# Low words of w_out of the first token chunk's first six blocks read from the tile that made them

## The chip, the cores and the metric

The kernel runs on one core of one Trainium2 chip. The metric is device time in microseconds (us), the median of several executions. An instruction stream goes to each engine: TensorE (PE, its weight loads shown as PEld), VectorE (DVE), ScalarE (ACT), GpSimd (POOL) and SyncE (SP). SP issues every data transfer of this kernel, one after the other.

## The reference

Three layers in a row on 2304 tokens (4 batches of 576) and 512 features:

```
scores = q k^T / sqrt(64);  bias = -(cum[:, None] - cum[None, :]), cum = cumsum(max(s, 0))
x   = softmax(causal(scores + min(bias, 0))) v          # 8 heads of 64
x   = ((x @ w_a) * (x @ w_b)) @ w_out                   # 512 -> 1536 -> 512
out = relu(x @ w_in)^2 @ w_out2                         # 512 -> 2048 -> 512
```

The weights arrive as 64-bit numbers. The kernel turns each block of them into a 32-bit number and splits that into a high and a low word; a product is then the sum of three matmuls: high weight by high x, high weight by low x, low weight by high x.

## The kernel before, in words

**Tiling.** The 1536 hidden features of the middle layer are 12 blocks f of 128 (`NF1`), in four groups of three (`GRP = 3`, `NG = 4`). Tokens are cut into chunks; chunk 0 is the first 512 tokens, all of batch 0. `moe1(c)` lists the steps of a chunk: `fstep(f)` multiplies x by blocks f of w_a and w_b (PSUM tiles `ab`), multiplies both results and splits the product into g high and low. After each third block, `ystep(grp, z)`, z = 0 and 1, multiplies the three g of a group by the matching rows of w_out, for output features d = 2z and 2z + 1 (PSUM tile `py`, nine matmuls for each d, three of them with low words). All fsteps and ysteps of chunk 0 run while attention of batch 1 runs, and their matmuls lie between its score (`st`), transpose (`pt`) and value (`av`) matmuls.

**Making the weights.** Just ahead of `fstep(f)` of chunk 0, `split_w(f)` loads the raw words of the blocks f of w_a, w_b and w_out (512 KB each, into five lent raw buffers, shown as roomxh, roomxl, words), decodes them on ACT, DVE and POOL, and writes the high words to a tile `wh` that stays for later chunks. The low words go to a tile too, and from there to memory: w_a's and w_b's to `wlab`, w_out's in two transfers of 128 KB to `wlo[g][z]` (lines 988 to 991). Later chunks load them from there.

**Where low words live.** The tag `wh` is a ring of 36 tiles (`3 * NF1`, line 962). The 36 high tiles keep theirs. On loan from it until all are made are: the low tiles of w_a and w_b of f < 5 (`LF`), the low tiles of w_out of f < 6 (`LF1 = 6`, line 971), and one decode tile for each of the first nine blocks of w_out (line 975). That is 36 + 10 + 6 + 9 = 61 takings, and they are served strictly in the order of first use: the 37th needs one tile back, the 61st needs 25 back. In chunk 0, `fstep` reads the low words of w_a and w_b from the tile that `split_w` made (`first_lo`); `ystep` does not, it loads w_out's low words back from `wlo` into a `loo` tile of 384 KB (two buffers), lines 1061 and 1062.

**What sets the order.** Nothing is ordered by hand. Every step only adds operations with reads and writes; `Plan.order` (line 148) then simulates the engines with fixed costs and writes out one order for each. A load costs 3 ns for each KB on its one transfer clock, 560 ns of SP's time, and its data count as there 2000 ns after its end (`LATE`); SP is let at most 3000 ns ahead of that transfer clock (`QUEUE`). PE prefers attention of batch 1 (stream `next`) to chunk 0's steps (`moe`). Where it sees PE idle, it fills in dummy matmuls: up to 40 named `glow`, and before a bank that waits over 400 ns some on that bank (`op.idle`, shown as L256). Each engine then runs its list strictly in order and waits where something is late.

Of the kernel before, what the change touches and what calls it, by code (L numbers as in the profile page):

```python
# [7 lines left out]
F32 = mybir.dt.float32  # L8
F32R = mybir.dt.float32r
# [7 lines left out]
P = 128  # L17
# [246 lines left out]
def attention_moe_moe(tc, q, k, v, s, w_a, w_b, w_out, w_in2, w_out2, out):  # L264
# [12 lines left out]
    GRP = 3  # L277
# [10 lines left out]
    LF1 = 6  # L288
# [28 lines left out]
    def pool(name):  # L317
        return lambda: pools[name]
# [4 lines left out]
    def sb(shape, dtype, tag, bufs, name):  # L323
        return pl.tile(pool("sb"), shape, dtype, tag, bufs, name)

    def at(shape, dtype, tag, bufs, name):
        return gated("at", shape, dtype, tag, bufs, name)

    def scratch(shape, dtype, name):
        return pl.fixed(lambda: pools["dram"].tile(shape, dtype, name=name))  # L330

    def mm_bank(name):
        return pl.tile(pool("mm"), [P, 512], F32, "mm", 3, name)
# [23 lines left out]
    def dve(*args, reads=(), **kw):  # L357
        pl.call(on_dve(*args, **kw), reads=reads)

    def act(*args, **kw):  # L360
        pl.call(on_act(*args, **kw))
# [4 lines left out]
    def dma(out, in_, kb, takes=(), lag=0.0):  # L366
        pl.call(("SP", kb * 3.0, False, "dma_start", (out, in_), {}), takes=takes, lag=lag)
# [26 lines left out]
    wlo = [scratch([HD, P, 2, GRP, P], F32, f"wlo{g}") for g in range(NG)]  # L394
# [420 lines left out]
    def new_x(nm):  # L815
        ts = [sb([P, ND, W], F32R, t, 1, f"{t}{nm}") for t in ("xh", "xl")]
        return lambda d, o, n: [t[:, d, o : o + n].part((d, o)) for t in ts]

    def split_x(x, d, o, n, pieces):

        xh, xl = x(d, o, n)
        for at_, m, src in pieces:
            dma(xl[:, at_ : at_ + m].bitcast(F32), src, m * 0.5)
        copy(n, xh, xl.bitcast(F32))
        subtract(n, xl, xl.bitcast(F32), xh.bitcast(F32))
# [31 lines left out]
    def decode(w, by_col, f, hi, lo, raw, t, takes, by):  # L857

        words(w, by_col, f, raw, t, takes)
        n = ND * P  # L860
        hi, lo = (x.rearrange("p d c -> p (d c)") for x in (hi, lo))
        copy(n, hi, t.bitcast(F32), by="A")
        subtract(n, lo, t.bitcast(F32), hi.bitcast(F32), by=by)
# [85 lines left out]

        quarters(w_out2, False, j, temp, "w2o", send, apart)  # L950

    wh, first_lo = {}, {}
    more = [at([P, 2, S], I32, "T1", NT1, f"words{i}").rearrange("p i s -> p (i s)")[:, : 2 * DM] for i in range(NT1)]
    room = [sb([P, ND, W], I32, t, 1, f"room{t}").rearrange("p d s -> p (d s)") for t in ("xh", "xl")]
    W8 = 2 * DM
# [3 lines left out]
    def split_w(f):  # L959
        def g():  # L960
            def spare(i):
                return sb([P, ND, P], F32R, "wh", 3 * NF1, f"wl{f}_{i}")

            ab = None if f < LF else sb([P, 2, ND, P], F32R, "lo", 3, f"wl{f}")
            first_lo[f] = []
            for i, w in enumerate((w_a, w_b, w_out)):
                hi = sb([P, ND, P], F32R, "wh", 3 * NF1, f"wh{f}_{i}")
                if i < 2:
                    lo = ab[:, i].part(i) if ab else spare(i)
                else:  # L970
                    lo = spare(i) if f < LF1 else sb([P, ND, P], F32R, "lo1", 1, f"wlo{f}")
                k_ = 3 * f + i
                t = ts[k_ % 2]
                if f < 9:
                    t = sb([P, DM], I32, "wh", 3 * NF1, f"wt{f}_{i}") if i == 2 else ts[i]
                lent = [*raws, *more] if k_ < MORE else raws
                decode(w, i < 2, f, hi, lo, lent[k_ % len(lent)], t, (), "PD")
                wh[f, i] = hi
                if i < 2:
                    first_lo[f].append(lo)  # L980
                    if f < LF:
                        dma(wlab[f][:, i].part(i), lo.bitcast(F32), 256, lag=LAG)
            if f >= LF:
                dma(wlab[f], ab.bitcast(F32), 512, lag=LAG)
            g_, r = divmod(f, GRP)
            for z in range(HD):
                dma(
                    wlo[g_][z][:, :, r, :].part((z, r)), lo[:, 2 * z : 2 * z + 2, :].bitcast(F32), 128, lag=LAG,
                )

        return g


    def halves(nm, dtype):
        t = sb([P, 2 * W], dtype, "g", GB, nm)
        return [t[:, z * W : z * W + W].part(z) for z in range(2)]
# [3 lines left out]
    def attended(d, l, r):  # L1000

        for b in range(B):
            g0, g1 = (FIRST if b == 0 else b * S), b * S + S
            a, z = max(l, g0), min(r, g1)
            if a < z:
                yield a - l, z - a, xd[b][0][d][:, a - g0 : z - g0].part(d)

    def moe1(c):
        steps = []
        t0, t1 = spans[c]  # L1010
        n = t1 - t0
        st = {}
        first_chunk = c == 0

        def load():
            if first_chunk:
                st["x"] = first_x
                return
            st["x"] = new_x(f"{c}")
            for d in range(ND):  # L1020
                split_x(st["x"], d, 0, n, list(attended(d, t0, t1)))

        steps.append(load)

        def fstep(f):
            def g():
                nm = f"{c}_{f}"
                if first_chunk:
                    lo = first_lo[f]
                else:  # L1030
                    lo = sb([P, 2, ND, P], F32R, "lo", 3, f"lo{nm}")
                    dma(lo.bitcast(F32), wlab[f], 512)
                gh, gl = (x[:, :n] for x in halves(f"g{nm}", F32R))
                st["g", f] = (gh, gl)
                pp = []
                for i in range(2):
                    ps = mm_bank(f"ab{nm}_{i}")[:, :n]
                    pairs = []
                    for d in range(ND):
                        xh, xl = st["x"](d, 0, n)  # L1040
                        li = lo[i][:, d, :] if first_chunk else lo[:, i, d, :]
                        pairs += [(wh[f, i][:, d, :], xh), (wh[f, i][:, d, :], xl), (li, xh)]
                    if f < PIECES:
                        for d in range(ND):
                            matmul(ps, n, pairs[3 * d : 3 * d + 3], d == 0)
                    else:
                        matmul(ps, n, pairs)
                    pp.append(ps)
                a_sb = sb([P, 512], F32, "a", 2, f"a{nm}")[:, :n]
                act("copy", n, a_sb, pp[0], psum=True)  # L1050
                pb = pp[1]
                dve("tensor_tensor", n, out=pb, in0=pb, in1=a_sb, op=ALU.mult)
                act("copy", n, gh, pb, psum=True)
                dve("tensor_tensor", n, out=gl, in0=pb, in1=gh.bitcast(F32), op=ALU.subtract)

            return g

        def ystep(grp, z):
            def g():
                nm = f"{c}_{grp}_{z}"  # L1060
                lo = sb([P, 2, GRP, P], F32R, "loo", 2, f"loo{nm}")
                dma(lo.bitcast(F32), wlo[grp][z], 384)
                for d in (2 * z, 2 * z + 1):
                    if grp == 0:
                        st["y", d] = sb([P, W], F32, f"y{d}", 1, f"y{nm}_{d}")[:, :n]
                    y = st["y", d]
                    ps = mm_bank(f"py{nm}_{d}")[:, :n]
                    pairs = []
                    for i in range(GRP):
                        f = grp * GRP + i  # L1070
                        gh, gl = st["g", f]
                        pairs += [(wh[f, 2][:, d, :], gh), (wh[f, 2][:, d, :], gl), (lo[:, d % 2, i, :], gh)]
                    matmul(ps, n, pairs)
                    if grp == 0:
                        copy(n, y, ps, psum=True)
                    else:
                        dve("tensor_tensor", n, out=y, in0=ps, in1=y, op=ALU.add)
                    if grp == NG - 1:
                        dma(yd[c][d].part(d), y, n * 0.5)

            return g


        for f in range(NF1):
            steps.append(fstep(f))
            if f == 0:
                steps.extend(tail)
                tail.clear()
            elif f % GRP == 0:
                steps.extend(ystep(f // GRP - 1, z) for z in range(HD))  # L1090
        last = [ystep(NG - 1, z) for z in range(HD)]
        (tail if t1 > (B - 1) * S - CC else steps).extend(last)
        return steps
# [506 lines left out]
```

## Time and profile before

| | |
|---|---|
| time, median of 3 executions | 1021.84 us (1020.78 to 1024.65) |
| the profiled execution's own time | 1023.91 us |
| its span, first to last instruction | 1022.1 us |
| PE busy | 1002.8 us, 98% |
| DVE, ACT, POOL busy | 735.5, 603.9, 322.3 us |
| transfers, hardware queue | 239.52 MB, 71.1% of 16 DMA engines' span |
| loads into `loo` in chunks 0 and later (384 KB each) | 24 |

Busy time counts each engine's own instructions. A wait row names the engine that idled, the instruction that it idled before, and whose event came last. In a timeline the bracket at a row's end is the idle time before it and what ended it. SPq is the stretch in which SP issues a transfer.

### The profile page before, as it was taken

The page shows a single profiled execution, that of the slowest core. Times are in us where ns is not written, and L with a number is a line of the kernel's source. Part 1 is how long each engine was busy: PE and PEld are TensorE (multiplying, and loading weights), DVE is VectorE, ACT ScalarE, POOL GpSimd, SP SyncE. Part 2 cuts the span into 40 slices and gives each one's busy share as a digit, 9 for nine tenths or more (in the row PEclk, how much of TensorE's full clock was granted, in tenths as well). Part 3 has the DMA queues.
Part 4 walks back from the last instruction along what each step waited for, and adds up shares of the span by engine and source line. Part 5 has one row for each costly group of instructions (what it writes and reads, how often), then busy time and mean ns, then how long its engine had stood idle before and what let it go on. Part 6 is the DMA issues. An engine that isn't in the chain of part 4 may idle for free.

```text
span 1022.1 us, 16764 instructions
## 1 busy us (share of the span) xinstructions
PE 1002.8 (98%) x5612; PEld 867.8 (85%) x5619; DVE 735.5 (72%) x1546; ACT 603.9 (59%) x1373; POOL 322.3 (32%) x293
## 2 busy tenths in 40 slices
PE   9999999999999999999999999999999999999997
PEld 5766777777777778788889999999999999999997
DVE  5878876756677765565697898688767755876566
ACT  6777886565777643343344544487565766657552
POOL 2243134325454622101122323323335212431123
PEclk9999999999999999999999999999999999999999
DMA  7458896558778667857666668499968876678664
GB/s 226 131 157 256 273 288 186 152 150 258 228 199 246 185 212 262 275 183 233 206 207 207 208 206 273 164 336 363 344 219 322 313 260 231 246 273 319 220 233 165
DMA packets 138006, 240.58 MB, mean 235 GB/s; under 512 B 21320, under 2 KB 91072, under 8 KB 137920
## 3 DMA queue, kind: packets, MB, share of 16 engines
q1 hardware_dynamic: 137920, 239.52, 71.1%
q8 instruction: 44, 0.72, 0.3%
q14 instruction: 42, 0.34, 0.1%
HBM read 181.42 MB, written 52.11 MB: 228 GB/s over the span
## 4 chain that ended last, share of the span: by engine, by line
PE 75%; DMA 5%; DVE 2%; SPq 1%; ACT 1%; issue 0%; DVEq 0%; ACTq 0%
PE ab L261 14%; PE pa L261 9%; PE py L261 8%; PE po_0t L261 6%; PE pw L261 5%; PE pc L261 5%; PE wa L261 4%; PE st L261 3%; PE av L261 3%; PE pt L261 3%; PE wc L261 2%; PE pb L261 2%; PE po_2b L261 2%; PE po_1b L261 2%; PE po_0b L261 2%; PE po_3b L261 2%
## 5 line engine op out<-in xcount | busy, mean ns | idle before, releaser
L261 ACT ACTIVATE e<-st,neg 120x336 f32<-120x336 f32 (+2 forms) x192 | 93.5, 492 | 28.5 <-DVE neg L261 26.6
L261 PE MATMUL py<-g,wh 128*128 128x512 f32 x288 | 92.0, 401 | 1.4 <-DVE y L261 1.2
L261 PE MATMUL ab<-xh,wh 128*128 128x512 f32 x192 | 77.4, 403 | 0.0
L261 PE MATMUL ab<-xh,lo 128*128 128x512 f32 x192 | 75.0, 391 | 0.0
L261 PE MATMUL ab<-xl,wh 128*128 128x512 f32 x192 | 75.0, 390 | 0.0
L261 PE MATMUL pt<-ident,e 120*120 120x120 f32 (+2 forms) x480 | 68.0, 268 | 0.8 <-DVE ph L261 0.4
L261 PEld LDWEIGHTS pt<-ident,e 120*120 120x120 f32 (+2 forms) x480 | 51.2, 133 | 20.2 <-issue 9.2
L261 DVE CUSTOM_DVE_ANT_0 st<-st,mask 96x96 f32<-96x96 f32 (+4 forms) x120 | 53.7, 453 | 20.0 <-PE st L261 18.2
L261 PE MATMUL ab<-x,wh 128*128 128x512 f32 x192 | 65.8, 424 | 0.8 <-ACT a L261 0.7
L261 PEld LDWEIGHTS py<-g,wh 128*128 128x128 f32 x288 | 53.3, 190 | 12.6 <-DVE y L261 1.6
L261 PE MATMUL av<-ph,val 120*64 120x240 f32 (+3 forms) x512 | 58.7, 360 | 0.0
L261 PE MATMUL st<-fk,fq 65*120 65x336 f32 (+2 forms) x192 | 56.3, 408 | 1.7 <-ACT e L261 1.7
L261 ACT COPY ph<-pt 120x360 f32<-120x360 f32 (+3 forms) x81 | 36.5, 459 | 35.9 <-PE pt L261 34.8
L261 PE MATMUL py<-g,loo 128*128 128x512 f32 x144 | 56.9, 395 | 0.0
L261 PEld LDWEIGHTS av<-ph,val 120*64 120x64 f32 (+1 forms) x512 | 31.1, 136 | 24.9 <-issue 12.4
L261 DVE COPY ph<-pt 120x360 f32<-120x360 f32 (+3 forms) x79 | 39.8, 514 | 16.2 <-PE pt L261 14.9
L261 DVE TENSOR_TENSOR ab<-ab,a 128x512 f32<-128x512 f32 x36 | 25.2, 701 | 33.3 <-PE ab L261 28.7
L261 PEld LDWEIGHTS ab<-xh,lo 128*128 128x128 f32 x192 | 36.0, 188 | 7.7
L261 ACT COPY a<-ab 128x512 f32<-128x512 f32 x36 | 21.1, 586 | 35.7 <-PE ab L261 35.6
L261 PEld LDWEIGHTS ab<-xh,wh 128*128 128x128 f32 x192 | 36.1, 188 | 6.4 <-issue 0.4
L261 PEld LDWEIGHTS ab<-x,wh 128*128 128x128 f32 x192 | 33.7, 189 | 9.2 <-ACT a L261 1.6
L261 PEld LDWEIGHTS ab<-xl,wh 128*128 128x128 f32 x192 | 36.2, 188 | 5.9
(692 smaller groups left out, 3098.4 us busy)
## 6 DMA issues: line engine op xcount, KB each, us to landing
w<-w2q SPq DMA_DIRECT2D x48, 896.0 KB, 6.7
lo<-wlab SPq DMA_DIRECT2D x36, 512.0 KB, 4.7
w2q<-w2ip SPq DMA_DIRECT2D x48, 256.0 KB, 4.2
w2s<-w2op SPq DMA_DIRECT2D x48, 256.0 KB, 4.6
loo<-wlo SPq DMA_DIRECT2D x24, 384.0 KB, 5.5
w2ir<-in_moe_w_in SPq DMA_DIRECT2D x16, 512.0 KB, 5.7
w2or<-in_moe_w_out SPq DMA_DIRECT2D x16, 512.0 KB, 4.3
ws_0t<-w2s SPq DMA_DIRECT2D x12, 512.0 KB
```

The lines of the kernel that those rows point to most:

```text
L261: getattr(eng, method)(*map(real, args), **{k: real(a) for k, a in kw.items()})
```

## The change

`split_w(f)` keeps the low tile of w_out of f < 6 in a list. In chunk 0 the two ysteps of groups 0 and 1 read their low words from these tiles; they make no `loo` tile and issue no load. Groups 2 and 3 of chunk 0, and all groups of later chunks, load as before. The transfers that write `wlo` stay.

```diff
-    wh, first_lo = {}, {}
+    wh, first_lo, first_out = {}, {}, {}
...
                 wh[f, i] = hi
+                if i == 2 and f < LF1:
+                    first_out[f] = lo
...
         def ystep(grp, z):
             def g():
                 nm = f"{c}_{grp}_{z}"
-                lo = sb([P, 2, GRP, P], F32R, "loo", 2, f"loo{nm}")
-                dma(lo.bitcast(F32), wlo[grp][z], 384)
+                near = first_chunk and grp * GRP + GRP <= LF1
+                if not near:
+                    lo = sb([P, 2, GRP, P], F32R, "loo", 2, f"loo{nm}")
+                    dma(lo.bitcast(F32), wlo[grp][z], 384)
...
-                        pairs += [(wh[f, 2][:, d, :], gh), (wh[f, 2][:, d, :], gl), (lo[:, d % 2, i, :], gh)]
+                        low = first_out[f][:, d, :] if near else lo[:, d % 2, i, :]
+                        pairs += [(wh[f, 2][:, d, :], gh), (wh[f, 2][:, d, :], gl), (low, gh)]
```

## Rows read from the trace of the kernel before

**Rows 1.** The page's first part: span, and each engine's busy time (share) and instructions.
```profile
span 1022.1 us, 16764 instructions
PE 1002.8 (98%) x5612; PEld 867.8 (85%) x5619; DVE 735.5 (72%) x1546; ACT 603.9 (59%) x1373; POOL 322.3 (32%) x293
```

**Rows 2.** PE's longest waits, 80 to 260 us: total us, times, longest.
```profile
PE st L261 <- ACT e L261: 3.8, 3, 2.1
PE st L261 <- DMA t2k<-T: 1.1, 1, 1.1
PE ab L261 <- ACT a L261: 0.7, 1, 0.7
```

**Rows 3.** Stretches: length, engines' busy us (instructions), PE clock, DMA share, GB/s.
```profile
97.00:102.00 5.00, 5.00 (x30) 3.19 (x31) 4.94 (x12) 4.07 (x9) 2.57 (x2) 1.00 1.02 333
120.00:140.00 20.00, 19.02 (x91) 13.63 (x91) 15.52 (x35) 14.28 (x32) 3.23 (x3) 1.00 0.98 306
240.00:245.00 5.00, 4.23 (x17) 3.54 (x18) 3.15 (x13) 4.53 (x14) 3.73 (x3) 0.76 0.51 173
```

**Rows 4.** SP's timeline: start, us, instruction, transfer.
```profile
92.80 0.48 SPq L261 DMA_DIRECT2D loo<-wlo  x1
...
121.98 0.86 SPq L261 DMA_DIRECT2D loo<-wlo  x2
...
123.81 0.40 SPq L261 DMA_DIRECT2D roomxh<-in_moe_w_b  x1
...
126.96 0.35 SPq L261 DMA_DIRECT2D roomxh<-in_moe_w_out  x1
```

**Rows 5.** SP's own waits, 117 to 128 us.
```profile
SPq L261 <- DMA wlo<-wl: 1.3, 1, 1.3
SPq L261 <- DMA loo<-wlo: 1.3, 2, 0.8
```

**Rows 6.** Transfers issued between 80 and 130 us: KB each, median us to landing.
```profile
loo<-wlo SPq DMA_DIRECT2D x4, 384.0 KB, 5.5
```

**Rows 7.** PE's timeline around groups 0 and 1 of chunk 0.
```profile
103.04 0.63 PE L261 MATMUL py<-g,wh 128*128 128x512 f32 x2
103.51 0.39 PE L261 MATMUL py<-g,loo 128*128 128x512 f32 x1
...
132.04 0.75 PE L261 MATMUL st<-fk,fq 65*120 65x288 f32 x2 [0.86 <-ACT e L261]
...
140.20 0.39 PE L261 MATMUL py<-g,loo 128*128 128x512 f32 x1
...
151.27 0.40 PE L261 MATMUL py<-g,loo 128*128 128x512 f32 x1
```

**Rows 8.** PE's groups, 117 to 142 us: count, busy us, mean ns, idle.
```profile
L261 PE MATMUL ab<-x,wl 128*128 128x512 f32 x24 | 9.5, 395 | 0.0
L261 PE MATMUL py<-g,loo 128*128 128x512 f32 x3 | 1.2, 395 | 0.0
L261 PE MATMUL glow<-warm 128*128 128x512 bf16 x3 | 1.0, 383 | 0.1
L256 PE MATMUL py<-warm 128*128 128x512 bf16 x2 | 0.6, 386 | 0.0
```

**Rows 9.** ACT's timeline in chunk 0.
```profile
130.99 0.68 ACT L261 ACTIVATE roomxh<-roomxh 128x512 f32<-128x512 f32 x1 [1.37 <-DMA roomxh<-in_moe_w_b]
131.56 0.33 ACT L261 ACTIVATE e<-st,neg 96x96 f32<-96x96 f32 x1
...
134.71 0.68 ACT L261 ACTIVATE roomxh<-roomxh 128x512 f32<-128x512 f32 x1 [1.17 <-DMA roomxh<-in_moe_w_out]
...
178.27 0.62 ACT L261 CAST wh<-roomxl 128x512 fp32r<-128x512 f32 x1
```

**Rows 10.** PE's timeline in chunk 1.
```profile
240.77 0.47 PE L261 MATMUL st<-T 66*120 66x456 f32 x1 [2.08 <-ACT e L261]
...
242.92 1.06 PE L261 MATMUL py<-g,wh 128*128 128x512 f32 x2
```

## The prediction

> **What bounds the kernel now.** I read the page's busy times first. PE works 1002.8 of 1022.1 us, so only 19.3 us are not PE's work [rows 1]. The change takes no matmul away; it can give back only idle time of PE, or dummy matmuls. The view of PE's waits comes next, cut to 80 to 260 us, where chunk 0 and the start of chunk 1 run: the three lines shown make 3.8 + 1.1 + 0.7 = 5.6 us, and nearly all of it is score matmuls (`st`) that wait for ACT's exponentials or for a transfer [rows 2]. No line of that view names `loo`. Then the stretches: from 97 to 102 us the transfers fill the DMA engines (share 1.02) and PE is busy 5.00 of 5.00; from 120 to 140 us the share is 0.98 and PE lacks 0.98 us [rows 3]. So the transfers are dense where the loads go, but only the second place shows at PE.
>
> **Part by part.** *The matmuls.* Two groups by four features d by three blocks are 24 matmuls that take their weights from another tile. In this very stretch a matmul with weights from `loo` has a mean of 395 ns, one with weights from a low tile on the ring, as `fstep` reads them, 395 ns too [rows 8]. Cost 0.
>
> *The loads themselves.* Four loads go, each 384 KB, 1.57 MB in all. The later one of group 0 is issued at 92.80 us and lands after a median of 5.5 us, at about 98.3; the first matmul that reads such a tile starts at 103.51 [rows 4, 6, 7]. The pair of group 1 is issued from 121.98 to 122.84 and lands by about 128.3; its first reader starts at 140.20 [rows 4, 6, 7]. So they are 5 and 12 us early, and what hides them is the matmuls of `fstep` and attention. Taking them away gives PE nothing directly.
>
> *What stands behind the loads.* SP issues in order. Ahead of group 1's pair SP waited 1.3 us for the `wlo` writes to land, which only these loads need, the pair took 0.86 us to issue, and later issues waited 1.3 us for `loo` loads to land [rows 4, 5]. Behind the pair stand w_b's raw words (123.81) and w_out's (126.96) [rows 4]. They could go up to 1.3 + 0.86 = 2.2 us and 2.2 + 1.3 = 3.5 us earlier, if their raw buffers are free by then, and they no longer share the engines with 2 x 384 KB, which at the 306 GB/s of that stretch is 2.6 us [rows 3]. ACT stood 1.37 us for w_b's words at 130.99; the exponentials of attention sit behind that instruction in ACT's list, and PE's score matmul at 132.04 idled 0.86 us for them [rows 7, 9]. Words that land 2.2 us earlier take the whole 1.37 us away, and with it the 0.86. Next late would be ACT's wait of 1.17 us for w_out's words at 134.71; no PE wait stands behind that one now, and the same shift moves it [rows 9]. Upper bound: the 0.86 and the five dummy matmuls in this stretch, which mark where the order expected PE idle, 1.0 + 0.6 us busy, so 2.5 us [rows 7, 8]. Lower bound 0, if the buffers come free no earlier. I take the row itself, 0.86. Behind group 0's loads PE was fully busy, so I count nothing there.
>
> *The ring.* The six low tiles stay taken until the last matmul of their group instead of until their write to `wlo` has landed. Up to block 8 the ring is served by the nine decode tiles and the ten low tiles of w_a and w_b. Block 9 ends with the 55th taking and needs 19 back, just these 19. Block 10 ends with the 58th, needs 22, and so must have group 0's three. Block 11's first high tile is the 59th, needs 23, and so must wait for group 1's last matmul, which starts at 151.27 [rows 7]. That tile is the 34th high tile and is written at 178.27 [rows 9], 26.6 us after group 1's end. Cost 0 at this cover; if group 1 came more than 26.6 us later, ACT's cast would wait for it, us for us, with the exponentials behind it.
>
> *The order.* The planner's transfer clock loses 4 x 384 x 3 ns = 4.6 us and SP's planned time 4 x 0.56 = 2.2 us, and `ystep` of groups 0 and 1 no longer waits in the plan for a load and its 2 us. All that follows is placed anew, transfers first. PE's work stays, the waits are dealt again. Bounds: all 5.6 us of [rows 2] go, and the clock loss of 240 to 245 us with them ((1 - 0.76) x 5 = 1.2 us [rows 3]); or as much comes on top. I take 0, since nothing in the rows gives this a sign.
>
> Sum: 0 + 0 - 0.86 + 0 + 0. The profiled execution took 1023.91 us, 1.81 outside its span and 2.07 above the median; it would take 1023.05. On the median, 1021.84 - 0.86 = 1021.0 us.
>
> **Rivals.** *Hidden anyway.* No row has PE wait for `loo`, and the raw words may be bound by their buffers, which decoding frees, not by SP. Then nothing moves: 1021.8 us. Against it: SP's 1.3 + 0.86 + 1.3 us between one load of raw words and the next, and ACT's 1.37 us [rows 4, 5, 9]. The Trainium skill, page "DMA: Bandwidth & Descriptors", section "Rules for kernel authors", says the same in general: a transfer issued early and waited for late has its cost overlapped by compute; by that rule the sum would be 0. The trace agrees for the loads (5 and 12 us early) but shows others waiting behind them.
>
> *Slower: a wait dealt to a worse place.* In chunk 1 ACT's list ran into a late transfer, PE's score matmul at 240.77 idled 2.08 us, and then the clock was 0.76 on average from 240 to 245: two `py` matmuls took 1.06 us where the same pair takes 0.63 [rows 3, 7, 10]. One such event is 2.08 + 1.2 = 3.3 us. If the new order lets chunk 0 end earlier, batch 2's preparation and chunk 1's loads move up against the last raw words. The rival decides from two more such events on: 1021.8 + 6.6 = 1028.4 us. For it: the stretch has little cover left, since ACT, DVE and transfers are all busy. Against it: four transfers fewer make the planned transfer clock more honest, and PE has attention to put in. The same skill's page "TensorE: Matmul & The Clock Gate", section "HAM oscillation", describes this price, waits for data that bring the clock to half so that the next work starts slow; the trace shows it after the 2.08 us wait and not after the 0.86.
>
> *Faster: chunk 0 unblocks.* If the freed transfers take out most waits from 80 to 260 us, up to 5.6 + 1.2 + 1.6 (dummies) = 8.4 us could go, 1013.4 us; three quarters of it is 6.3, 1015.5 us. For it: several of the waits end with an ACT that was behind a transfer. Against it: the largest (240.77) lies 100 us behind the loads.
>
> *It doesn't do what it says.* The new test is 0 + 3 <= 6 and 3 + 3 <= 6, so groups 0 and 1 both pass and four loads must go; only if the ring stalled as above would the place be another. 1021.8 us or above.
>
> **How the numbers follow.** Forecast (1018.8 to 1023 on its own) 0.42; hidden anyway 0.20; slower by events 0.20; faster by a re-dealt chunk 0.14; not doing what it says 0.04. About 0.5%, 5.1 us, is what a measurement of this kernel can tell from no change. Faster than 1016.7 is the faster case, 0.14. Above 1026.9 lies most of the slower case, 0.16 of 0.20. The rest, 0.70, is no change. The range must reach into both outer cases: from 1014.5, short of the full 8.4, to 1028.5, two such events.
>
> **What would show it.** Right: 20 `loo` loads of 384 KB in place of 24; w_b's raw words of the sixth or seventh block issued without a wait for `wlo` ahead of them; ACT's wait for them under 0.5 us; no PE wait before `st` near 132 us; PE's busy time within 2 us of 1002.8; the cast of the 34th high tile well behind group 1's last `py`. Wrong: the same ACT wait with the loads gone (then buffers set it), a low tile waited for by ACT or POOL, or new PE waits between 150 and 260 us with a clock under 1.00 that outweigh the 0.86.

## The result and the profile after

The changed kernel takes 1030.74 us (median of 6 runs, 1026.95 to 1036.32) against 1020.85 us for the kernel before beside it: ratio 1.0098, 95% interval 1.0072 to 1.0125. That is slower by some 10 us, outside the predicted range, on the side that had a chance of 0.16. The profiled execution took 1028.86 us with a span of 1027.1. The same kernel timed again later gave 1031.97 us, ratio 1.0120 (1.0098 to 1.0142), span 1032.4.

The page's first part, to be read against [rows 1]: span, then busy time of each engine.

```profile
span 1027.1 us, 16727 instructions
PE 1002.8 (98%) x5619; PEld 867.3 (84%) x5619; DVE 740.0 (72%) x1557; ACT 600.2 (58%) x1365; POOL 326.4 (32%) x290
```

PE's busy time is what it was, 1002.8 us: in this profile the span grew by 5.0 us, and all of that is PE standing idle. (In the second profile PE is busy 1005.0 of 1032.4 us, so 27.4 us are idle in place of 19.3.) The planner also picks the engine of an operation that several of DVE, ACT and POOL can do: DVE has 11 instructions more than before, ACT 8 and POOL 3 fewer [rows 1]. What I call the order below is the planner's whole output, sequence and engine; no run here separates the two. The transfers fell from 239.52 to 237.94 MB and the 384 KB loads into `loo` from 24 to 20, so the change does what it says.

Next, where PE idles now. PE's longest waits from 80 to 260 us, against [rows 2]:

```profile
PE st L261 <- ACT e L261: 3.1, 2, 1.9
PE ab L261 <- ACT a L261: 1.1, 1, 1.1
PE py L261 <- DVE g L261: 1.0, 1, 1.0
PE pt L261 <- ACT e L261: 0.7, 1, 0.7
```

And the stretches, against [rows 3] (length, PE, PEld, DVE, ACT, POOL busy, PE clock, DMA share, GB/s):

```profile
120.00:140.00 20.00, 18.12 (x87) 12.89 (x85) 14.74 (x34) 14.10 (x34) 4.99 (x4) 1.00 0.87 263
140.00:160.00 20.00, 17.02 (x72) 12.70 (x71) 17.02 (x40) 11.74 (x26) 5.23 (x5) 0.91 0.74 252
240.00:245.00 5.00, 5.00 (x30) 4.09 (x27) 3.67 (x14) 3.70 (x10) 3.28 (x3) 1.00 0.40 126
```

In this profile the hole at 240 us is gone (5.00 of 5.00, clock 1.00). In its place PE lacks 1.9 us from 120 to 140 and 3.0 us from 140 to 160 with a granted clock of 0.91, though the DMA engines are less full than before (0.87 against 0.98). Chunk 0 now has the holes that chunk 1 had, and more of them. The second profile of the same kernel has them in both chunks: in chunk 1 PE waits 2.03 us before an `st` at 252.01, for a transfer, and the clock is low:

```profile
250.00:255.00 5.00, 2.99 (x15) 1.96 (x15) 0.90 (x4) 1.76 (x7) 4.53 (x7) 0.65 0.87 299
255.00:260.00 5.00, 5.00 (x28) 3.67 (x24) 2.60 (x10) 1.47 (x4) 0.56 (x1) 0.67 0.82 242
```

What makes them is read from SP and ACT. SP's timeline (start, us, transfer), against [rows 4], and its two longest waits from 117 to 140 us, against [rows 5]:

```profile
123.08 0.82 SPq L261 DMA_DIRECT2D val<-in_v  x2
...
124.44 0.39 SPq L261 DMA_DIRECT2D roomxh<-in_moe_w_b  x1
...
126.20 0.61 SPq L261 DMA_DIRECT2D roomxh<-in_moe_w_out  x1
...
135.36 0.33 SPq L261 DMA_DIRECT2D xd<-u  x1
135.96 0.38 SPq L261 DMA_DIRECT2D words<-in_moe_w_b  x1
136.63 0.34 SPq L261 DMA_DIRECT2D words<-in_moe_w_out  x1
```

```profile
SPq L261 <- DVE u L261: 3.1, 1, 3.1
SPq L261 <- PE rs L261: 2.4, 1, 2.4
```

The two `loo` loads are gone from 121.98, but w_b's words go out at 124.44, 0.63 us later than before (0.16 us of it stand between the two profiles at 117 us already): SP stands 2.4 us for PE's `rs`, which the `val` loads need, and both of these now stand ahead of w_b's words (before, one stood ahead and one behind). Further down SP stands 3.1 us for `u` to store it to `xd`, with the next block's words of w_b and w_out behind that store. In the kernel before, the same three issues have the other order:

```profile
133.72 0.38 SPq L261 DMA_DIRECT2D words<-in_moe_w_b  x1
134.69 0.34 SPq L261 DMA_DIRECT2D words<-in_moe_w_out  x1
136.32 0.34 SPq L261 DMA_DIRECT2D xd<-u  x1
```

ACT's timeline after, against [rows 9]:

```profile
130.94 0.68 ACT L261 ACTIVATE roomxh<-roomxh 128x512 f32<-128x512 f32 x1 [1.69 <-DMA roomxh<-in_moe_w_b]
...
133.67 0.66 ACT L261 ACTIVATE roomxh<-roomxh 128x512 f32<-128x512 f32 x1 [1.24 <-DMA roomxh<-in_moe_w_out]
...
144.45 0.66 ACT L261 ACTIVATE words<-words 128x512 f32<-128x512 f32 x1 [3.92 <-DMA words<-in_moe_w_out]
```

And PE's timeline, against [rows 7]:

```profile
132.49 0.75 PE L261 MATMUL st<-fk,fq 65*120 65x288 f32 x2 [1.15 <-ACT e L261]
...
142.57 0.40 PE L261 MATMUL py<-g,wl 128*128 128x512 f32 x1
...
146.31 1.11 PE L261 MATMUL st<-fk,fq 65*120 65x216 f32 x4 [1.95 <-ACT e L261]
147.04 1.09 PE L261 MATMUL py<-g,wh 128*128 128x512 f32 x2
...
152.09 0.73 PE L261 MATMUL py<-g,wh 128*128 128x512 f32 x2 [1.03 <-DVE g L261]
...
156.08 0.39 PE L261 MATMUL py<-g,wl 128*128 128x512 f32 x1
```

In this profile one chain joins them: `xd` waits for `u` (3.1 us), the words behind it come late, ACT stands 3.92 us for them with attention's exponentials behind, and PE's `st` idles 1.95 us. Then a pair of `py` takes 1.09 us in place of 0.63, at a clock of 0.74 from 145 to 150. In the second profile SP's wait for `u` (4.2 us) and ACT's for w_out's words (2.4 us) are there again, but PE's long wait in chunk 0 is another, for DVE:

```profile
149.93 0.73 PE L261 MATMUL py<-g,wh 128*128 128x512 f32 x2 [2.65 <-DVE g L261]
```

Summed from 80 to 1000 us (PE idle, plus length times one minus the clock, from slices of 20 us; each column is one profile):

| stretch, us | before | after | after, second profile |
|---|---|---|---|
| 80 to 160 | 1.9 | 6.0 + 1.8 | 6.3 |
| 160 to 260 | 4.0 + 1.8 | 0.7 | 3.0 + 3.4 |
| 260 to 500 | 0.1 | 1.7 | 2.7 |
| 500 to 660 | 2.2 | 2.4 | 2.4 |
| 660 to 740 | 2.2 | 4.4 | 4.5 |
| 740 to 1000 | 1.3 | 0.9 | 0.9 |

So three places are worse in both profiles: chunk 0, the stretch about 325 us, where PE's `rs` waits for ACT's `ph` (1.2 us, 2.0 in the second profile), and 700 to 710 us, where `po_0t` waits 2.6 us in two waits for its weights (2.7). The last lies over 550 us behind the last load taken away, so the suspect is the order and not the loads.

How far the order moved can be counted from the plans alone, by running `Plan.order` of the two kernels without the chip. One operation of the plan, such as a chain of matmuls into one tile, is one entry. Outside the longest sequence that an engine's lists before and after share lie 203 of PE's 1248 entries, 377 of DVE's 1437, 241 of ACT's 1172, 83 of POOL's 286 and 193 of SP's 788; 269 of the 1452 operations with a choice of engine go to another one. In the traces the engines' lists differ up to about 740 us.

The same simulation gives each plan an end of its own: 998.5 us before, 1005.8 us after. With four transfers fewer, the plan itself comes out 7.3 us longer.

### The profile page after: what moved, and what is told of

The parts are those of the page before. It is cut to its first block, busy times and chain, and to the rows that moved or that the text cites. A ratio compares the mean times of both kernels' runs of the same rounds, so it can differ in the third digit from the quotient of the medians.

```text
span 1027.1 us, 16727 instructions
## 1 busy us (share of the span) xinstructions
PE 1002.8 (98%) x5619; PEld 867.3 (84%) x5619; DVE 740.0 (72%) x1557; ACT 600.2 (58%) x1365; POOL 326.4 (32%) x290
## 3 DMA queue, kind: packets, MB, share of 16 engines
q1 hardware_dynamic: 137344, 237.94, 70.2%
## 4 chain that ended last, share of the span: by engine, by line
PE 90%; DMA 5%; DVE 2%; ACT 1%; SPq 1%; issue 0%; DVEq 0%; ACTq 0%
PE ab L261 18%; PE pa L261 9%; PE py L261 9%; PE st L261 7%; PE po_0t L261 6%; PE av L261 5%; PE wa L261 5%; PE pt L261 5%; PE pc L261 5%; PE pw L261 5%; PE wc L261 2%; PE pb L261 2%; PE po_1b L261 2%; PE po_2b L261 2%; PE po_0b L261 2%; PE po_3b L261 2%
## 5 line engine op out<-in xcount | busy, mean ns | idle before, releaser
L261 ACT ACTIVATE e<-st,neg 120x216 f32<-120x216 f32 (+2 forms) x192 | 93.3, 491 | 28.7 <-DVE neg L261 26.8
L261 PE MATMUL py<-g,loo 128*128 128x512 f32 x120 | 46.9, 391 | 0.0
L261 DVE TENSOR_TENSOR y<-py,y 128x512 f32<-128x512 f32 x36 | 24.8, 689 | 24.6 <-PE py L261 24.6
L261 PEld LDWEIGHTS st<-fk,fq 65*120 65x120 f32 x192 | 30.0, 180 | 14.6 <-ACT e L261 4.0
```

What stands on the lines that cost most here:

```text
L261: getattr(eng, method)(*map(real, args), **{k: real(a) for k, a in kw.items()})
```

## The experiments

The first runs separate the two things that the diff does: it changes where 24 matmuls read (the data), and it changes what the planner counts (the order).

**The old order with the new data.** The four loads stay in the plan at their full cost but are not issued; the 24 matmuls read the tiles. All five engines keep the order of before; the lists in the traces differ in the 24 matmuls and the four missing loads alone. (`Other(a, b)` counts as `a` in the plan and reads `b`.)

```diff
                 dma(lo.bitcast(F32), wlo[grp][z], 384)
+                near = first_chunk and grp * GRP + GRP <= LF1
+                if near:
+                    pl.ops[-1].ways["SP"] = (1152.0, [], False)
...
-                        pairs += [..., (lo[:, d % 2, i, :], gh)]
+                        pairs += [..., (Other(lo, first_out[f][:, d, :]) if near else lo[:, d % 2, i, :], gh)]
```

> All engines keep the order of the kernel before; only the 24 low-word matmuls of groups 0 and 1 read the tiles that made the words, and the four loads are not issued (the planner still counts them). Theory A (the time comes with the order that the planner deals anew): as before, ratio 0.997 to 1.002, about 1020 us, with ACT's wait near 131 us and PE's 0.86 us shorter. Rival B (the data path itself: ring tiles held longer, traffic and waits that the four loads had spread out): slower as the change is, ratio 1.007 to 1.012, about 1030 us.

Measured: 1019.32 us (12 runs), ratio 0.9983 (0.9964 to 1.0002). The data alone cost nothing that shows, and may bring 0.17%. PE has hardly a wait left in chunk 0 (idle from 80 to 160 us: 0.3 in place of 1.9). Its waits there are this one line:

```profile
PE ab L270 <- ACT a L270: 0.2, 1, 0.2
```

From 660 to 740 us PE idles 4.25 us in this profile all the same and loses 1.8 us to the clock, with 2.4 us in one wait for `w<-w2q`. So idle time there comes with the old order too, and tells little by itself.

The timelines of SP and then of ACT in this kernel:

```profile
121.67 0.34 SPq L270 DMA_DIRECT2D val<-in_v  x1
122.21 0.30 SPq L270 DMA_DIRECT2D rd<-rows  x1
122.60 0.39 SPq L270 DMA_DIRECT2D roomxh<-in_moe_w_b  x1
...
124.92 0.61 SPq L270 DMA_DIRECT2D roomxh<-in_moe_w_out  x1
```

```profile
128.26 0.68 ACT L270 ACTIVATE roomxh<-roomxh 128x512 f32<-128x512 f32 x1
...
131.84 0.67 ACT L270 ACTIVATE roomxh<-roomxh 128x512 f32<-128x512 f32 x1 [1.03 <-DMA roomxh<-in_moe_w_out]
```

ACT's 1.37 us for w_b's words and PE's 0.86 are gone, as forecast, but only half for the reason forecast. SP did not win its 2.2 us: where it waited and issued `loo`, it now waits for PE's `rs`. w_b's words go out 1.21 us earlier, and an offset of 0.76 us stood between the two profiles at 85 us already. What changed is the transfer itself: issued at 123.81 and awaited until 130.99 before (7.2 us), issued at 122.60 and in place by 128.26 now (at most 5.7 us). The Trainium skill, page "DMA: Bandwidth & Descriptors", section "Rules for kernel authors", says that transfers share the same 16 engines; this pair of durations, with and without 2 x 384 KB beside it, agrees.

**The new order with the old data.** After's order on all engines, with the four loads issued again where before has them in SP's list, and the matmuls reading the loaded copy.

```diff
+    def bring(g_):
+        for z in range(HD):
+            back[g_, z] = sb([P, 2, GRP, P], F32R, "loo", 2, f"back{g_}{z}")
+            hold(pl.ops[-1], back[g_, z].buf)
+            pl.ops[-1].ways["SP"][1].append(("dma_start", (back[g_, z].bitcast(F32), wlo[g_][z]), {}))
...
+                        if (f, i) == (3, 1):
+                            bring(0)
...
+                if f == 6:
+                    bring(1)
```

> All engines keep the order of the changed kernel; the four loads are issued again, at the places in SP's list where the kernel before has them, and the 24 matmuls read them. A: slow as the change is, ratio 1.006 to 1.014, 1027 to 1035 us. B: back at the time before, ratio 0.998 to 1.003.

Measured: 1031.37 us (6 runs), ratio 1.0120 (1.0097 to 1.0143), against 1.0120 for the changed kernel beside it. The loads can come back and nothing that shows gets worse or better.

> The changed kernel once more, for a second profile and for the spread: ratio 1.007 to 1.0125 by both theories. A expects the new waits of PE (146 us behind ACT's wait for raw words, and 694 to 708 us) to return in the same places, since the order is fixed.

Measured: 1031.97 us (6 runs), ratio 1.0120 (1.0098 to 1.0142). The wait at 700 to 710 us returned; the one near 146 us did not, and 2.65 us at 149.93, for DVE, came in its place.

The four corners:

| | order of before | order of after |
|---|---|---|
| loaded copy | 1 | 1.0120 (1.0097 to 1.0143) |
| tile read where it is | 0.9983 (0.9964 to 1.0002) | 1.0120 (1.0098 to 1.0142) |

The whole loss goes with the order, and none that shows with the data.

**The order from the plan's cost alone.** Before, with every load issued and read, but the four loads counted as 300 KB, then as 0 KB, on the planner's transfer clock.

```diff
-                dma(lo.bitcast(F32), wlo[grp][z], 384)
+                dma(lo.bitcast(F32), wlo[grp][z], 300 if first_chunk and grp < 2 else 384)
```

> The kernel before, same loads and same matmuls; the planner alone counts 300 KB instead of 384 for the four loads, which deals the order anew from about 110 us to 650 us. A: the time moves with no change of data, to either side, by 0.3 to 1.2% (1009 to 1033 us). B: no move, ratio 0.998 to 1.002.

> The kernel before, same loads and matmuls; the planner alone counts 0 KB for the four loads on its transfer clock (SP's 560 ns each stay). Theory A (a newly dealt order moves the time by itself): off by 0.3 to 1.2% to either side, slower the likelier, since loads_costed_300 was 1.0037; rival B (only the changed kernel's order is bad, by accident of these places): within 0.998 to 1.003.

Measured: 300 KB 1.0037 (1.0019 to 1.0054); 0 KB 1.0074 (1.0053 to 1.0095). A kernel that does just what before does is slower by 0.7% when four numbers in its plan are changed.

**Mending single places of the new order.** Two transfers that the traces accuse were moved in SP's list of the changed kernel: the store `xd<-u` behind the two loads of words, and eight stores of second-stage weights behind the `ws_0t` loads that `po_0t` waits for; then both.

```diff
+        behind("fixed<-u:u1_0", "T1:words1<-in")
...
+        for x in ("00", "10", "01", "11"):
+            behind(f"fixed<-wh:w2op7_{x}", "lo:ws0_0t3<-fixed")
+        for x in ("20", "21", "30", "31"):
+            behind(f"fixed<-wh:w2op7_{x}", "lo:ws0_0t2<-fixed")
```

> The changed kernel with one move in SP's list: the store of batch 1's first u to memory goes behind the two loads of raw words that follow it (it waits for DVE's u, which waits for the reciprocals' transfers). Theory A1 (this store holds the raw words up, ACT then waits for them ahead of attention's exponentials, and PE idles and drops its clock between 120 and 160 us): ACT's wait of 3.92 us near 144 us falls under 1 us, PE's idle time from 120 to 160 us from 5 to 1 or 2 us, ratio to before 1.006 to 1.009 in place of 1.012. Rival B1 (ACT, DVE and transfers are too full there; the wait only moves): 1.010 to 1.013, and PE's idle time of that stretch stays at 4 us or more.

> The changed kernel with eight stores of split w_out2 words (the last block's) moved in SP's list behind the two ws_0t loads that they stand ahead of, as they stand in the kernel before. A2 (PE's 2.6 us wait for ws_0t at 697 to 708 us is these stores' waits for ACT): the wait falls under 1 us, ratio to before 1.008 to 1.011. Rival B2 (the loads wait for their buffers, or the transfers are full there, share 1.02): the wait stays over 2 us, 1.011 to 1.013.

> Both moves together. A1 and A2: their gains add, ratio to before 1.003 to 1.007. B1 and B2: 1.010 to 1.013. If one holds, the sum is that one's.

Measured: 1.0100 (1.0078 to 1.0122), 1.0123 (1.0099 to 1.0147) and 1.0117 (1.0093 to 1.0141): no gain that shows from any, as the rivals B1 and B2 expected. With the `xd` store moved, ACT's wait of 3.92 us shrank to 0.21 (ACT's timeline), but PE still idles 4.0 us from 120 to 160 us (4.9 in the first profile of the change), for it waited 2.35 us a little later, for DVE's `g` (PE's timeline), while DVE was busy 5.00 of 5.00 us (the stretch):

```profile
140.38 0.71 ACT L283 ACTIVATE words<-words 128x512 f32<-128x512 f32 x1 [0.21 <-DMA words<-in_moe_w_out]
```

```profile
149.00 0.95 PE L283 MATMUL py<-g,wh 128*128 128x512 f32 x2 [2.35 <-DVE g L283]
```

```profile
145.00:150.00 5.00, 2.65 (x11) 1.89 (x10) 5.00 (x14) 3.21 (x6) 2.06 (x2) 0.93 0.81 257
```

This wait for `g` is PE's longest from 80 to 160 us in every profile of the new order but the first, where it was 1.0 us: 2.6 in the second, 2.8 with the loads back, and 2.3, 3.0 and 3.2 in the three kernels here. In the kernel before PE has no wait for `g` there. What stands ahead of `g` in DVE's list was not moved in any run, so this suspect is untested.

With the other stores moved, `po_0t` still waits, and from 685 to 712 us SP stands longest for PE's `po_0b`, which by the trace gives a buffer of these weights back (5.9 us; 3.5 before the move). PE's waits from 660 to 740 us, then SP's own from 685 to 712 us (total, times, longest):

```profile
PE po_0t L286 <- DMA ws_0t<-w2s: 3.5, 2, 2.6
```

```profile
SPq L286 <- PE po_0b L286: 5.9, 3, 2.8
```

So of the two places, one wait of ACT could be taken out and gave nothing back, since PE's next wait, for DVE, comes at nearly the same time; the other wait stayed.

**More or less cost in the plan.** Is the lost cost a margin, of which more is better, or was the old order only a good one among many? Four more values.

> The kernel before with one number changed: the planner counts the four loads of groups 0 and 1 as 340 KB instead of 384 on its transfer clock; every load and its data stay. Theory M (the four loads' planned cost was a margin that kept transfers apart; less of it is worse, in proportion): between the 300 KB run (1.0037) and no change, so about 1.002. Theory L (the old order was a good draw among many; any re-deal loses, with no direction): anywhere from 1.000 to 1.012, no relation to the 300 KB run; most likely 1.004 to 1.007.

> The kernel before, the four loads counted as 430 KB instead of 384. Theory M (margin): at or under 1.000, more margin is no worse. Theory L (a good draw): 1.003 to 1.012, as slow as the draws with less cost.

> The kernel before, the four loads counted as 480 KB instead of 384. Theory M (margin): at or under 1.000. Theory L (a good draw): 1.003 to 1.012, with no order by the number.

> The kernel before, the four loads counted as 768 KB, twice what they are. Theory M (margin): not above 1.002; the planner now holds transfers back by 4.6 us of its clock, as much as the change gave away. Theory L (a good draw): 1.003 to 1.012 as with any other number; a mirror image of costing them at 0 (1.0074).

Measured, with the earlier values, the entries outside the sequence shared with before, summed over the five engines, and the end that the planner's own simulation gives:

| KB counted | ratio (95%) | entries moved | plan's own end, us |
|---|---|---|---|
| 0 | 1.0074 (1.0053 to 1.0095) | 1012 | 1006.4 |
| 300 | 1.0037 (1.0019 to 1.0054) | 601 | 1001.7 |
| 340 | 1.0014 (0.9995 to 1.0033) | 586 | 999.6 |
| 384 (before) | 1 | 0 | 998.5 |
| 430 | 1.0037 (1.0018 to 1.0055) | 612 | 1003.6 |
| 480 | 1.0050 (1.0030 to 1.0069) | 817 | 1002.3 |
| 768 | 1.0085 (1.0058 to 1.0113) | 917 | 1001.5 |
| after (loads not planned) | 1.0098 and 1.0120 | 1097 | 1005.8 |

The margin falls: 430, 480 and 768 KB should have been no slower, and are; only 340 KB came out where it said, at about 1.002. That the old order is a good one among many stands, with a correction. Its expectation said that there is no relation to the number; yet the ratio rises with the distance from 384 on both sides, and nearly with the count of moved entries. All seven other orders that the planner dealt have a ratio above 1, and in six of them the interval excludes 1. In the planner's own simulation all seven end later too, by 1.1 to 7.8 us: the sign is right each time, the size within 0.15% for five, and too small for 768 KB (0.30%) and for the change (0.73%).

## Why the prediction was wrong

- *The matmuls, 0.* Right: 397 ns with weights from the low tile from 140 to 146 us, where the clock was full, against 395 [rows 8], and PE busy 1002.8 both times.
- *The loads themselves, 0.* Right: without them the ratio is 0.9983 (0.9964 to 1.0002) in the one order and the same 1.0120 as with them in the other.
- *What stands behind the loads, -0.86.* Right in the order of before, where the wait of PE is gone and 1 - 0.86 / 1021 = 0.9992 lies in the interval (so does 1, and the time alone would not tell); the issue time that I put first did not carry it, the shorter transfer did. In the order that the change brings it did not come at all: ACT waits 1.69 us at 130.94 and PE 1.15 at 132.49.
- *The ring, 0.* Right: group 1's last `py` starts at 156.08, and no ACT cast to a high tile waits for it; the casts to high tiles that stand about where the 34th did start at 176.41, 20 us behind.
- *The order, 0.* This is the step that failed: "I take 0, since nothing in the rows gives this a sign". It measured +1.0 to +1.2%, 10 to 12 us, and its bound of 5.6 + 1.2 = 6.8 us was too narrow as well, because I took it from one stretch, 80 to 260 us, while the order was dealt anew as far as about 740 us.
- *The sign.* The rows gave none, but the planner did: its own simulation ends 7.3 us later with the change, and 1021.84 + 7.3 = 1029.1 us would have been nearer to the measured 1030.74 than anything in the sum. I never asked it. That a list at 98% [rows 1] has little left to win fits the seven slower orders, but it is an argument after the fact.
- *The rivals.* "A wait dealt to a worse place" named the mechanism of the first profile: a late transfer ahead of ACT, an idle `st`, then half the clock, and its price per event, 3.3 us, is near the 1.95 + 1.8 measured at 146.31. It had the place half wrong (in chunk 1 the first profile has no such event and the second has one, at 252.01; both have them in chunk 0, which it did not name) and the number too small: three places or more, not two events. What I held against it, that fewer transfers make the plan more honest, fell with the 0 KB and 300 KB runs only in part: those plans are less honest and slower, but the changed kernel's plan is honest, slowest, and nearly the longest in the planner's own simulation.

What stays open: why the plan gets longer with fewer transfers, how much of the loss is the sequence and how much the choice of engine, and where the changed kernel loses 3 to 5 us more than its plan. No single entry was found that makes the difference, and the count of moved entries and the plan's end only go along with the loss; neither was varied by itself.

## What to carry to other kernels

Where a planner with fixed costs writes the order, an edit that takes out planned work is two edits: time each by itself, by leaving the cost in the plan while nothing is issued. Before any run, let the planner simulate both plans and compare their ends: here that had the sign right for all seven new orders. Bound a re-deal over all that is dealt anew, not over the stretch of the edit. A wait found in the trace of a slower kernel is a suspect only: take it out and see whether the time comes back; here two were taken on, one went, and no time came back. And profile a kernel twice before reading its waits: two profiles of one fixed order had PE's long wait in chunk 0 end with different engines.

## What the runs showed of the hardware

A wait of PE of about 2 to 3 us cost a second time by the clock in some cases and not in others: after 1.95 us (146.31) it was 0.74 from 145 to 150 us and 0.91 from 150 to 155, and after the 2.35 us wait in the kernel with the `xd` store moved 0.72 from 150 to 155; after 2.65 us at 149.93 in the second profile of the changed kernel it stayed at 1.00, and so it did after 3.19 us at 149.73 in the kernel with both moves. The 2.03 us wait at 252.01 in that second profile cost most, 0.65 from 250 to 255 us and 0.67 from 255 to 260, 3.4 us of clock. The lost 1.8 us are thus no fixed part of such a wait.
